# A Fourier transform and a top-1 mixture of experts in one kernel: the third batch's list in 19 blocks of 128, transforms that end eight blocks ahead, and the third batch's last part beside the list of two batches

## The chip, the cores and the metric

One NeuronCore of one Trainium2 chip runs the whole program. The metric is device time in microseconds (us). Engines: TensorE (PE, matmuls, and PEld for its weight loads), VectorE (DVE), ScalarE (ACT), GpSimd (POOL, which issues the indirect DMAs), SyncE (SP, which issues all other DMAs). Each engine works through its own instructions strictly in the order in which the program was built, so an instruction that waits holds back all that stands behind it on its engine.

## The reference

```python
def _attn_ref(x):                      # x: 8 x 2496 x 256
    X = np.fft.fft(x, axis=1)
    X = np.fft.fft(X, axis=2)
    return X.real.astype(np.float32)

def _moe_ref(x, modality_id, w_gate, modality_bias, w1, w2):   # x: 19968 x 256, 8 experts, F = 1024
    logits = x @ w_gate + modality_bias[modality_id]
    e_idx = np.argmax(logits, axis=1)
    probs = softmax(logits)
    gate_w = probs[np.arange(N), e_idx]
    for e in range(E):
        mask = e_idx == e
        h = np.maximum(x[mask] @ w1[e], 0.0)
        out[mask] = gate_w[mask, None] * (h @ w2[e])
```

Each of 8 batches of 2496 rows is Fourier transformed in both directions; each resulting row then goes through the one expert with the highest logit, two layers of 256 x 1024 and 1024 x 256.

## The kernel before, in words

**Transforms.** The transform of a batch is written as matmuls. Its input is loaded (`load_x`, L359) in two halves XM, folded on DVE (`fold`, L441 to L476), and put through `stage1` (L489, matmuls L506 or L508) and `stage23` (L515), which for each of 11 groups g makes a stage-2 product T2 (matmuls L532, L537 or L540) and, one group later, a stage-3 product (matmuls L550 or L552). Batches 0 to 2 use fp32 matmuls, batches 3 to 7 pairs of fp16 numbers (a high and a low part). Every product leaves PSUM in an evacuation: where pairs are made, ACT writes the high part (L486) and DVE the low part (L487). Of a stage-3 product, the 512 values of a row go into a row tile `rp` in this way, and the 16 gate logits are copied to `Lg` (L560). Six buffers (RPB) hold the `rp` tiles of even batches and batch 1.

**Routing.** `route` (L592) takes the logits to expert, gate weight and destination, on DVE for the most part. Each batch's rows are then scattered by 22 indirect DMAs on POOL (`scatter`, L669) into the HBM buffer `xd`, sorted by expert. Batch 0's are issued at once, those of later batches wait in a list `pend` and are issued a few at a time (`paced`, `trickle`).

**Weights.** `weights` (L775) loads each expert's fp32 weights (L802), and splits them into fp16 pairs on ACT and DVE (L812 to L844), which end up in SBUF and, by `wstore` (L797), in the HBM buffer `w16`.

**Expert blocks.** A block takes 256 or 128 rows of one expert (`block`, L963): SP loads the expert's weights from `w16` where they change (L987, L988), the rows transposed (xT, L990), and indices and gates (ig, L993). PE runs the first layer (L1006, 48 matmuls of 256 or 128 columns), ACT and DVE evacuate the hidden values H as fp16 pairs (L1011 and L1012; four evacuations a block of 256, two a block of 128), PE runs the second layer (L1024, 24 matmuls per 128 rows), ACT scales the result into a tile `ob` (L1030, two buffers) and POOL scatters it to the output (L1031, "outs").

Eight *speculative* blocks, one of 256 rows for each expert (`spec_blocks`), run as soon as batch 0 is routed, with the weights that have just been split. Then come *lists*: a list R takes as many full blocks as the rows of batches 0 to R-1 are sure to give (`table`, L875, on DVE). The first list, of two batches (R = 2), has blocks of 128 rows; the next six have 256; a last one takes what remains, in blocks of 128. While the blocks of list R run, the transforms of later batches are fed in between.

**What sets the order.** Python generators are stepped by hand. Up to the first list the string `SEQ` says which goes next: `w` a step of the weights, `s` a step of the transforms, `b` half a speculative block. In the lists, `knots` (L1056) reads from the points `pts` (L1113) how far the transforms (`k.pos`) should be after `at` units of 256 rows. A scheduler then places the instructions of each engine, with the order of stepping as priority.

Of the kernel before, what the change touches and what calls it, by code (L numbers as in the profile page):

```python
# [13 lines left out]
F32 = mybir.dt.float32  # L14
# [16 lines left out]
ROW = 516  # L31
RW = 516
CH = 3
RPB = 6
RPL = 4
HIP = ()
HIV = ()
# [19 lines left out]
NSLOT = 2  # L57
NS2 = 3
LEAD = 2
EARLY = -1  # L60
FIRST = 2
WAB = 4
WFB = 1
# [10 lines left out]
UB = 2  # L74
RV = 1
FG = 6
SEQ = "wsssssssswssssswssswsssssssssssssssssssssssssswssssbsswssswsssssbwsssssbsssssbwsssswsbwsswssswsssssbwbsssssbsssssbwsssssbwsssssbwsssssbwssssswwssssssssswssssswsssssssssss"
PARTS = ((0, 3), (3, 5))
XE = 1
M2 = 1  # L80
# [145 lines left out]
class Kernel:  # L226
# [288 lines left out]
    def stage23(self, b):  # L515
# [8 lines left out]
        for g in range(G + 1):  # L524
# [19 lines left out]
            if g > 0:  # L544
                T2 = T2s[g - 1]
                ps3 = self.psf.tile([P, 512], F32, name="psf")
                for j, cols in enumerate((slice(0, 145), slice(145, 280))):
                    if hl:
                        for k, (a, w) in enumerate(HL):
                            nc.tensor.matmul(ps3[0:M3, cols], self.e3h[:, a, j, :], T2[:, w, cols], start=k == 0, stop=k == 2)  # L550
                    else:
                        nc.tensor.matmul(ps3[0:M3, cols], self.e3[:, j, :], T2[:, cols], start=True, stop=True)  # L552
                j = (g - 1) % CH
                if j == 0:
                    pool, n = (self.rows, RPL) if b >= SPB and b % 2 else (self.rt, RPB)
                    self.rp.append(pool.tile([M3, CH, RW], I16, name="rp", bufs=n))
                row = self.rp[-1].bitcast(F16)[:, j, 0:512].rearrange("p (h s c) -> p h s c", h=2, c=64)
                seg = ps3[0:M3, 0:288].rearrange("p (s c) -> p s c", c=72)
                self.evac(row, seg[:, :, 0:64], 2.0 ** -20 if hl else self.inv[0][:M3])
                nc.vector.tensor_copy(Lg[:, g - 1], seg[:, 0:3:2, 64:72])  # L560
            yield

    def modality(self):
# [399 lines left out]
    def block(self, S, ti, i, o=0, n=0, ex=None):  # L963
# [62 lines left out]
        gs = p.tile([P, NT], F32, name=f"gs{S}", bufs=3)  # L1026
        V.tensor_scalar(gs, ig[:, :, 1], w2[:, 4 * F:4 * F + 2].bitcast(F32), None, ALU.mult)  # L1027
        for tg in range(NT):
            ob = p.tile([P, D], F32, name="ob", bufs=2)
            self.ob = nc.scalar.activation(ob, po[:, tg, :], AF.Identity, scale=gs[:, tg:tg + 1]).ins  # L1030
            ins = nc.gpsimd.indirect_dma_start(  # L1031
                out=t["out"], out_offset=bass.IndirectOffsetOnAxis(ap=ig.bitcast(I32)[:, tg, 0:1], axis=0),
                in_=ob, in_offset=None, bounds_check=TOK - 1, oob_is_err=False).ins
            tc.declare_no_dep(ins, group="out_w", reason="rows are disjoint")
            tc.add_to_no_dep_group("out_w", ins)
            if self.started:
                self.trickle(ins)
# [27 lines left out]
def fft_moe(ctx, tc, t):  # L1065
# [28 lines left out]
    k.w1.append(p.tile([P, 4 * F], F16, name="w1_y", bufs=1))  # L1094
    k.w2.append(p.tile([P, WROW - 4 * F], F16, name="w2_y", bufs=1))
    k.nslot = NS2
    while k.ready < R0 - 1:
        next(st, None)
    for _ in blk:
        k.paced()  # L1100
        for i in range(3):
            next(st, None)
            k.paced()
    k.started = True

    R0 = FIRST
    size = lambda R: P if R == R0 else 256
    starts, taken = {R0: 0}, k.ntaken
    for R in range(R0, B):
        n = (R * N - taken - E * (size(R) - 1)) // size(R)  # L1110
        starts[R + 1] = starts[R] + n * size(R) / 256
        taken += size(R) * n
    pts = [(0, k.pos)] + [(starts[b] + EARLY, b + 1) for b in range(SPB, B)]  # L1113
    at = 0
    k.slots = lambda b: int(2 * (starts[b + 1] - LEAD - at))
    tab = k.table(size(R0), False, R0)
    for R in range(R0, B + 1):
        blk, nxt = k.blocks(size(R), tab, R), None
        for _ in blk:
            at += size(R) / 512  # L1120
            while k.pos < knots(at, pts) and next(st, END) is not END:
                pass
            if R < B and nxt is None and at >= starts[R + 1] - LEAD:
                while k.ready < R:
                    next(st)
                nxt = k.table(256, False, R + 1)
        tab = nxt
    run_all([k.blocks(128, k.table(128, True))])

# [54 lines left out]
```

## Time and profile before

| | us |
|---|---|
| median of 3 runs (1081.33 to 1083.68) | 1083.2 |
| the profiled execution | 1081.88 |
| its span, first to last instruction | 1080.1 |
| PE busy (10128 matmuls) | 1007.7 |
| DVE busy | 552.8 |
| ACT busy | 446.8 |
| POOL busy | 373.3 |

The profile shows one execution. In its groups a row gives line, engine, operation, out<-in with their shapes, count, then busy time, mean ns of one, and the engine's idle time just before them with what ended it. In timelines a row is start, duration, engine, line, operation, count, and in brackets the idle time before it with its releaser. Matmuls overlap, so PE's busy time is not PE at its full rate. The granted TensorE clock is a share of full speed.

### The profile page before, as it was taken

What the parts mean: (1) busy time and instruction counts of PE and PEld (TensorE: products, weight loads), DVE (VectorE), ACT (ScalarE), POOL (GpSimd) and SP (SyncE); (2) the same over time, 40 slices, a digit from 0 to 9 for tenths busy, and PEclk for the clock granted to TensorE, in tenths of its full rate; (3) what the DMA queues carried; (4) which work ended last, traced back from release to release, by engine and by line L of the source; (5) the groups of instructions that cost most, each with busy time, mean ns of one, the idle gap of its engine ahead of it and who ended that gap; (6) DMA issues with size and microseconds to landing.
All of it is one profiled execution on the core that took longest, in us unless ns stands there. A gap on an engine that the chain in (4) does not pass through costs nothing.

```text
span 1080.1 us, 26648 instructions
## 1 busy us (share of the span) xinstructions
PE 1007.7 (93%) x10128; PEld 910.1 (84%) x10128; DVE 552.8 (51%) x1620; ACT 446.8 (41%) x882; POOL 373.3 (35%) x351
## 2 busy tenths in 40 slices
PE   6776879889998999999999999999999999999996
PEld 5656868779888988889899999888888888899985
DVE  4878888978887442363565334732222222222221
ACT  6755767744644333333443343332323233233221
POOL 0072482861243334343334333345543112121111
PEclk9897989999999999999999999999999999999998
DMA  9667987799497979877878595849976886797663
GB/s 348 246 227 247 308 270 240 260 295 332 135 287 226 305 240 292 225 235 249 252 221 259 178 251 156 244 126 287 298 215 197 244 272 183 222 242 204 163 156 105
DMA packets 156484, 254.89 MB, mean 236 GB/s; under 512 B 118364, under 2 KB 121317, under 8 KB 136125
## 3 DMA queue, kind: packets, MB, share of 16 engines
q1 hardware_dynamic: 136973, 210.96, 66.7%
q0 software_dynamic: 19376, 42.16, 11.8%
q8 instruction: 82, 1.34, 0.5%
q14 instruction: 53, 0.43, 0.1%
HBM read 231.59 MB, written 60.48 MB: 270 GB/s over the span
## 4 chain that ended last, share of the span: by engine, by line
PE 64%; issue 13%; DMA 9%; DVE 5%; ACT 4%; POOL 3%; SPq 1%; POOLq 0%; ACTq 0%; DVEq 0%
PE psm L1006 29%; PE pso L1024 28%; DMA XM<-x 3%; DMA out<-ob,ig 3%; POOL out L1031 2%; PE psf L550 2%; PE psf L532 1%; PE psf L506 1%; ACT wj L812 1%; DVE XM L368 1%; DMA xd<-rp,dsti 1%; PE psf L508 1%; POOL xd L670 1%; DMA wa<-w 1%; DVE w L838 1%
## 5 line engine op out<-in xcount | busy, mean ns | idle before, releaser
L1024 PEld LDWEIGHTS <-H 128*128 128x128 f16 x3864 | 376.1, 98 | 55.7 <-ACT H L1011 10.3
L1031 POOL DMA_INDIRECT out<-ob,ig x161 | 166.6, 1035 | 583.2 <-ACT ob L1030 503.4
L1012 DVE SCALAR_TENSOR_TENSOR H<-psm,H 128x512 f16<-128x512 f32 x322 | 218.4, 686 | 282.7 <-ACT H L1011 281.4
L1006 PE MATMUL psm<-xT,w 128*128 128x256 f16 (+1 forms) x3216 | 315.0, 256 | 13.5 <-DMA xT<-xd 6.7
L1024 PE MATMUL pso<-w,H 128*128 128x256 f16 x2616 | 308.0, 273 | 10.7 <-ACT H L1011 9.0
L1006 PEld LDWEIGHTS <-w 128*128 128x128 f16 x3216 | 268.9, 99 | 41.3 <-issue 11.7
L1011 ACT ACTIVATE H<-psm 128x512 f16<-128x512 f32 x322 | 190.5, 597 | 239.8 <-PE psm L1006 238.7
L1030 ACT ACTIVATE ob<-pso,gs 128x256 f32<-128x256 f32 x161 | 70.7, 471 | 282.1 <-PE pso L1024 239.4
L1006 PE MATMUL psm<-xT,w_y 128*128 128x256 f16 (+1 forms) x1440 | 135.3, 251 | 0.5 <-DVE H L1012 0.4
L670 POOL DMA_INDIRECT xd<-rp,dsti x88 | 104.7, 1190 | 84.5 <-DVE sp_i L863 53.7
L1024 PE MATMUL pso<-w_y,H 128*128 128x256 f16 x1152 | 133.3, 273 | 0.0
L1006 PEld LDWEIGHTS <-w_y 128*128 128x128 f16 x1440 | 117.0, 98 | 11.0 <-issue 1.2
L670 POOL DMA_INDIRECT xd<-rm,dsti x88 | 93.3, 1060 | 28.5 <-issue 25.2
L487 DVE SCALAR_TENSOR_TENSOR T<-psf,T 120x280 f16<-120x280 f32 (+2 forms) x95 | 43.2, 461 | 56.3 <-ACT T L486 55.9
L1027 DVE TENSOR_SCALAR gs<-ig,w 128x2 f32<-128x2 f32 (+1 forms) x67 | 15.2, 227 | 63.2 <-DMA ig<-xd 63.2
L486 ACT ACTIVATE T<-psf 120x280 f16<-120x280 f32 (+2 forms) x95 | 38.6, 421 | 15.4 <-PE psf L532 10.2
L812 ACT ACTIVATE wj<-wa 128x1024 f16<-128x1024 f32 x32 | 34.3, 1072 | 9.5 <-DMA wa<-w 9.4
L550 PE MATMUL psf<-T,pack 120*117 120x145 f16 x330 | 31.8, 224 | 4.8 <-DVE T L487 3.0
L368 DVE TENSOR_TENSOR XM<-XM 128x1280 f32<-128x1280 f32 (+2 forms) x18 | 24.1, 1338 | 23.2 <-DMA XM<-x 23.2
L552 PEld LDWEIGHTS psf<-T,pack 120*117 120x117 f32 x132 | 19.4, 188 | 17.0 <-ACT T L482 11.2
L552 PE MATMUL psf<-T,pack 120*117 120x145 f32 (+1 forms) x132 | 23.4, 300 | 11.1 <-ACT T L482 7.5
L532 PE MATMUL psf<-pack,T 128*120 128x144 f16 (+1 forms) x330 | 32.2, 229 | 1.3 <-DVE Lg L560 1.3
(197 smaller groups left out, 772.8 us busy)
## 6 DMA issues: line engine op xcount, KB each, us to landing
w<-w SPq DMA_DIRECT2D x67, 1028.0 KB
w<-w SPq DMA_DIRECT2D x67, 1024.0 KB
w_y<-w SPq DMA_DIRECT2D x30, 1028.0 KB
w_y<-w SPq DMA_DIRECT2D x30, 1024.0 KB
XM<-x SPq DMA_DIRECT2D x14, 1280.0 KB
wa<-w SPq DMA_DIRECT2D x16, 1024.0 KB
out<-ob,ig POOLq DMA_INDIRECT x161, 6.3
w<-w_x SPq DMA_DIRECT2D x2, 1028.0 KB
```

Of the source, the lines that this page charges most:

```text
L487: self.mark = self.nc.vector.scalar_tensor_tensor(dst[:, 1], ps, scale, dst[:, 0], ALU.mult, ALU.subtract).ins
L532: nc.tensor.matmul(oh, T1[h][:, a, g, :], self.m2h[h][:, w], start=h + k == 0, stop=h * k == 2, skip_group_check=True)
L550: nc.tensor.matmul(ps3[0:M3, cols], self.e3h[:, a, j, :], T2[:, w, cols], start=k == 0, stop=k == 2)
L552: nc.tensor.matmul(ps3[0:M3, cols], self.e3[:, j, :], T2[:, cols], start=True, stop=True)
L670: i = self.nc.gpsimd.indirect_dma_start(out=self.t["xd"], out_offset=bass.IndirectOffsetOnAxis(ap=at, axis=0), in_=row, in_offset=None, bo ...
L812: nc.scalar.activation(jk, x, AF.Square, accum_out=st[:, i:i + 1])
L1006: l1 = nc.tensor.matmul(ps[:, q, :], w1v[:, h, kt, ft], xT[:, xs, :], start=k == 0, stop=k == 5).ins
L1011: nc.scalar.activation(H[:, 0, f0:f0 + NF, :], ps, AF.Relu)
L1012: self.mark = V.scalar_tensor_tensor(H[:, 1, f0:f0 + NF, :], ps, 0.0, H[:, 0, f0:f0 + NF, :], ALU.max, ALU.subtract).ins
L1024: nc.tensor.matmul(po[:, tg, :], H[:, hh, ft, tg * P:(tg + 1) * P], w2v[:, wh, ft, :], start=k == 0, stop=k == 23)
L1030: self.ob = nc.scalar.activation(ob, po[:, tg, :], AF.Identity, scale=gs[:, tg:tg + 1]).ins
L1031: ins = nc.gpsimd.indirect_dma_start(out=t["out"], out_offset=bass.IndirectOffsetOnAxis(ap=ig.bitcast(I32)[:, tg, 0:1], axis=0), in_=ob, i ...
```

## The change

Five things are changed together. Lines below the constants are one higher in the changed file.

1. `SEQ` is shorter: 82 `s` steps instead of 136, and the last `b` and `w` steps stand close together. Before the first list, the old kernel stepped the transforms until three batches were routed (and three more steps for each remaining half block); the new one steps until two are (one step for each). The point (1, max(3, k.pos)) then lets the rest of the third batch be stepped within the first two blocks of the first list.
2. The list of three batches (R = 3) is cut into blocks of 128 too (`SMALL = 4`). By the counts of `starts`, the lists were 15 blocks of 128, then 5, 10, 10, 10, 9 and 10 of 256, then 22 of 128 for these inputs; they are now 15 and 19 of 128, then 6, 9, 10, 10 and 10 of 256, then 21 of 128.
3. A batch's transform now ends eight units before the start of the list that needs it (`AHEAD`), instead of one unit before the start of the list ahead of that.
4. The logit copy to `Lg` goes from DVE to ACT.
5. `ob` has four buffers instead of two, `rp` five instead of six.

```diff
-RPB = 6
+RPB = 5
...
-EARLY = -1
+AHEAD = 8
+SMALL = 4
...
-SEQ = "wsssssssswssssswssswsssssssssssssssssssssssssswssssbsswssswsssssbwsssssbsssssbwsssswsbwsswssswsssssbwbsssssbsssssbwsssssbwsssssbwsssssbwssssswwssssssssswssssswsssssssssss"
+SEQ = "wsssssssswssssswssswsssssssssssssssssssssssssswssssbsswssswsssssbwsssssbsssssbwsssswsbwsswssswsssssbwbsbbwbwbwbwwwww"
...
-                nc.vector.tensor_copy(Lg[:, g - 1], seg[:, 0:3:2, 64:72])
+                nc.scalar.copy(Lg[:, g - 1], seg[:, 0:3:2, 64:72])
...
-            ob = p.tile([P, D], F32, name="ob", bufs=2)
+            ob = p.tile([P, D], F32, name="ob", bufs=4)
...
-    while k.ready < R0 - 1:
-        next(st, None)
     for _ in blk:
         k.paced()
-        for i in range(3):
-            next(st, None)
-            k.paced()
+        next(st, None)
+        k.paced()
+    while k.ready < 1:
+        next(st, None)
...
-    size = lambda R: P if R == R0 else 256
+    size = lambda R: P if R < SMALL else 256
...
-    pts = [(0, k.pos)] + [(starts[b] + EARLY, b + 1) for b in range(SPB, B)]
+    pts = [(0, k.pos), (1, max(3, k.pos))] + [(starts[b + 1] - AHEAD, b + 1) for b in range(SPB, B)]
...
-                nxt = k.table(256, False, R + 1)
+                nxt = k.table(size(R + 1), False, R + 1)
```

**ACT, in the speculative blocks.** Before, around the two outs' evacuations of the fourth such block (`ob<-pso`, L1030; `wj` is a square sum of the weights, `T` and `rp` are evacuations of the transform, DMASW are POOL's DMAs):

```order
L1030 ACTIVATE ob<-pso,gs_1750 128x256 [waits DMASW0_49,PE_49]
L1030 ACTIVATE ob<-pso,gs_1750 128x256 [waits DMASW1_49]
L1011 ACTIVATE H_1798<-psm 128x512 [waits PE_49]
L812 ACTIVATE wj,wst<-wa 128x1024 [waits Activation_49]
L1011 ACTIVATE H_1798<-psm 128x512 [waits PE_49]
L486 ACTIVATE rp<-psf,xsc 117x256 [waits PE_49]
L542 COPY T_1605<-psf 120x280 [waits PE_49]
```

And the same block's place in the changed kernel:

```order
L1031 ACTIVATE ob<-pso,gs_1750 128x256 [waits PE_49]
L1031 ACTIVATE ob<-pso,gs_1750 128x256
L1012 ACTIVATE H_1798<-psm 128x512 x2
L487 ACTIVATE rp<-psf,xsc 117x256 [waits PE_49]
L543 COPY T_1605<-psf 120x280 [waits PE_49,Activation_49]
L1012 ACTIVATE H_1798<-psm 128x512 [waits PE_49]
L475 ACTIVATE XM<-Pt,xsc 128x640 [waits DVE_49]
L475 ACTIVATE XM<-Qt,xsc 128x640 [waits DVE_49]
L813 ACTIVATE wj,wst<-wa 128x1024 [waits Activation_49]
L487 ACTIVATE rp<-psf,xsc 117x256 [waits PE_49]
L561 COPY Lg<-psf 117x16 [waits DVE_49] x2
```

These two ob evacuations no longer wait for POOL's DMAs, and two logit copies, which wait for DVE, have come in behind a row's evacuation.

**DVE, at the first list block.** Before, from the gate scale `gs` of the first list block to its two evacuations (`H_3086`):

```order
L1027 TENSOR_SCALAR gs_3266<-ig_3084,w_0_106 128x1
L487 SCALAR_TENSOR_TENSOR T_2887<-psf,T_2887 120x280
L475 SCALAR_TENSOR_TENSOR XM<-Pt,xsc,XM 128x640
L475 SCALAR_TENSOR_TENSOR XM<-Qt,xsc,XM 128x640
L487 SCALAR_TENSOR_TENSOR rp<-psf,rp 117x256
L560 COPY Lg<-psf 117x16
L487 SCALAR_TENSOR_TENSOR T_2968<-psf,T_2968 120x280
L1012 SCALAR_TENSOR_TENSOR H_3086<-psm,H_3086 128x512
L487 SCALAR_TENSOR_TENSOR rp<-psf,rp 117x256
L560 COPY Lg<-psf 117x16
L1012 SCALAR_TENSOR_TENSOR H_3086<-psm,H_3086 128x512
```

In the changed kernel, around the same block's two (`H_2663`; L461 to L470 are half of a fold, here of batch 4's input):

```order
L462 TENSOR_TENSOR XM<-XM 128x635
L461 TENSOR_TENSOR XM<-XM 128x5x127
L466 COPY Qt<-XM 128x5
L468 TENSOR_TENSOR Pt<-XM 128x5x63
L470 TENSOR_TENSOR Qt<-XM 128x5x63
L465 COPY Pt<-XM 128x5
L467 TENSOR_TENSOR Pt<-XM 128x5x64
L469 TENSOR_TENSOR Qt<-XM 128x5x64
L1028 TENSOR_SCALAR gs_2863<-ig_2661,w_0_106 128x1
L1013 SCALAR_TENSOR_TENSOR H_2663<-psm,H_2663 128x512 x2
L488 SCALAR_TENSOR_TENSOR T_2978<-psf,T_2978 120x280
L369 TENSOR_TENSOR XM<-XM 128x1280
```

Before, the last T2 and row evacuations of batch 3 stood ahead of the first list block's H; now batch 3's T2 evacuations begin behind it, and the logit copies are gone from DVE.

More of the change, by code (lines that the diff above doesn't have):

```diff
@@ L1096, in fft_moe @@
     k.nslot = NS2
-    while k.ready < R0 - 1:
-        next(st, None)
     for _ in blk:
         k.paced()
-        for i in range(3):
-            next(st, None)
-            k.paced()
+        next(st, None)
+        k.paced()
+    print('POS', k.pos, len(k.pend))
+    while k.ready < 1:
+        next(st, None)
     k.started = True
     R0 = FIRST
-    size = lambda R: P if R == R0 else 256
+    size = lambda R: P if R < SMALL else 256
     starts, taken = {R0: 0}, k.ntaken
```

## The prediction

> **What bounds the kernel now.** I read the page's slices first, then three windows cut where the work changes (first speculative block, first list block, end of the first list, last matmul), then the waits and timelines of VectorE (DVE), ScalarE (ACT) and TensorE (PE) in the first of them. In the slices each digit is the busy share of 27 us in tenths; look at where PE reaches 9 and where DVE leaves 7 to 8.
>
> ```profile
> PE   6776879889998999999999999999999999999996
> DVE  4878888978887442363565334732222222222221
> ```
>
> The windows: busy time and, in brackets, instructions of each engine, then granted clock, DMA share, GB/s.
>
> ```profile
> 94.00:238.00 144.00, 125.82 (x1121) 110.24 (x1120) 121.64 (x372) 91.46 (x167) 76.92 (x58) 0.92 0.88 279
> 238.00:346.00 108.00, 100.44 (x1387) 95.65 (x1385) 93.45 (x323) 55.84 (x121) 32.29 (x29) 0.98 0.83 241
> 346.00:1071.00 725.00, 719.09 (x7297) 652.09 (x7296) 273.00 (x714) 238.60 (x472) 235.20 (x236) 1.00 0.79 226
> ```
>
> From 346 us on PE is busy 719 of 725 us: nothing is to be gained there but by less PE work. From 94 to 238 us the eight speculative blocks run beside the transforms of batches 2 and 3 and the weight preparation. DVE is busy 121.6 of 144 us there, ACT 91.5. PE is marked busy 125.8, but 768 MoE matmuls are only 84 us of it at the full rate that these chain rows give (start, us, what):
>
> ```profile
> 255.98 2.68 PE psm L1006 x48
> 258.66 2.62 PE pso L1024 x24
> ...
> 425.92 3.93 PE psm L1006 x36
> ...
> 432.14 4.26 PE pso L1024 x39
> ```
>
> A block of 128 is 2.68+2.62 = 5.30 us. Of a block of 256, 36 first-layer matmuls take 3.93 and 39 second-layer ones 4.26, so 0.109 us each and 10.48 for the 96. So the first 238 us hold the loss, and DVE is nearest to being the bound there. PE's total work hardly changes; the time falls by as much as the first list block starts earlier, less the PE work that is moved behind that start.
>
> **Part 1: DVE work that leaves the stretch before the first list block.** In the DVE order I counted between the first speculative block's H evacuation and the first list block's. Gone from there are 11 T2 evacuations, 9 row evacuations, 20 logit copies, 4 splits of L475 and half a batch's fold (L368, L460, L461, L466 to L469 once each).
>
> ```profile
> L487 DVE SCALAR_TENSOR_TENSOR T<-psf,T 120x280 f16<-120x280 f32 x55 | 24.1, 440 | 33.1 <-ACT T L486 32.9
> L487 DVE SCALAR_TENSOR_TENSOR rp<-psf,rp 117x256 f16<-117x256 f32 x55 | 22.8, 414 | 5.1 <-ACT rp L486 5.1
> L560 DVE COPY Lg<-psf 117x16 f32<-117x16 f32 x88 | 14.2, 161 | 0.0
> L475 DVE SCALAR_TENSOR_TENSOR XM<-Pt,xsc,XM 128x640 f16<-128x640 f32 x10 | 8.8, 880 | 1.1 <-ACT XM L474 0.9
> L368 DVE TENSOR_TENSOR XM<-XM 128x1280 f32<-128x1280 f32 x14 | 20.8, 1484 | 15.3 <-DMA XM<-x 15.3
> L460 DVE TENSOR_TENSOR XM<-XM 128x635 f32<-128x635 f32 x12 | 9.7, 808 | 0.0
> L466 DVE TENSOR_TENSOR Pt<-XM 128x320 f32<-128x320 f32 x12 | 5.8, 480 | 0.0
> ```
>
> 11 x 0.440 + 9 x 0.414 + 20 x 0.161 + 4 x 0.880 + (1.48 + 2 x 0.81 + 4 x 0.48) = 20.3 us. Neighbours on DVE overlap by some 0.06 us, which takes 3 us off, and about as much comes back from small pieces (a row copy, the steps of a table): 20 us, read as that much earlier since DVE hardly rests there. What goes later with them: 1 x load on SP, 20 scatters on GpSimd (POOL), and PE work, part 4.
>
> **Part 2: ob in four buffers.** Two outs of ob queue on POOL behind scatters, so ACT stands for a free ob, and behind it in ACT's order stand the H evacuations that DVE and PE wait for. ACT's rows, then DVE's:
>
> ```profile
> 155.08 0.47 ACT L1030 ACTIVATE ob<-pso,gs 128x256 f32<-128x256 f32 x1 [5.57 <-DMA out<-ob,ig]
> 156.69 0.47 ACT L1030 ACTIVATE ob<-pso,gs 128x256 f32<-128x256 f32 x1 [1.14 <-DMA out<-ob,ig]
> ...
> 225.75 0.47 ACT L1030 ACTIVATE ob<-pso,gs 128x256 f32<-128x256 f32 x1 [3.00 <-DMA out<-ob,ig]
> ```
>
> ```profile
> 157.69 0.69 DVE L1012 SCALAR_TENSOR_TENSOR H<-psm,H 128x512 f16<-128x512 f32 x1 [2.51 <-ACT H L1011]
> 159.21 0.69 DVE L1012 SCALAR_TENSOR_TENSOR H<-psm,H 128x512 f16<-128x512 f32 x1 [0.83 <-ACT H L1011]
> ...
> 226.75 1.30 DVE L1012 SCALAR_TENSOR_TENSOR H<-psm,H 128x512 f16<-128x512 f32 x2 [3.94 <-ACT H L1011]
> ```
>
> DVE idles 2.51+0.83+3.94 = 7.3 us for them. With four buffers an ob waits for the out of two blocks back, and the last speculative outs have almost no scatters ahead of them in the new POOL order. I take 7 us, bounds 0 and 7.3. Late next is what DVE lacks in the other 15 us of its idle time, the speculative blocks' ig loads and the weights' ScalarE half among it.
>
> These stalls also cool PE: in the window around the first one the clock is 0.86, and 12 first-layer matmuls take 2.77 us, 11 of them later 1.36.
>
> ```profile
> 135.00:162.00 27.00, 20.20 (x164) 17.83 (x162) 22.00 (x54) 17.12 (x32) 21.81 (x18) 0.86 0.90 271
> ```
>
> ```profile
> 161.89 2.77 PE L1006 MATMUL psm<-xT,w 128*128 128x256 f16 x12
> ...
> 168.60 1.36 PE L1006 MATMUL psm<-xT,w 128*128 128x256 f16 x11
> ```
>
> The Trainium skill, "TensorE: Matmul & The Clock Gate", section "Part 1: The HAM clock gate", says the clock falls to half after an idle window of about 3.4 us; the trace agrees in that the 2.77 us stand behind a wait of PE of 5 us for that H. By the rule the removed stall also gives back PE speed, at most 0.14 x 27 = 3.8 us here, and the sum would be that much lower if PE set the pace. DVE does, so my sum has nothing for it.
>
> **Part 3: the logit copy on ACT.** It is 0.16 us on DVE; on ACT it must wait until DVE has done its half of the same evacuation. Queued behind it on ACT are T2, row and H evacuations, and DVE, then PE, wait for those. ACT has 52 us free in the first window, so its own time costs nothing. In the new ACT order one to six instructions mostly stand between a row's evacuation and its copy, and DVE mostly has over 1 us of other work before it needs ACT's next piece; for eight or so of the 33 copies ahead of the first list it has less than ACT's pieces take (by the mean durations of the trace), by 7 us together. Bounds 0 and 7, I take +3. With parts 1 and 2 the first list block, now at 237.7, starts 24 us earlier, near 214.
>
> **Part 4: PE work moved and added.** Ahead of the first 128-column matmul PE's order had 60 stage-2 and 49 stage-3 matmuls of batch 3, and now 10 and 0; 28 second-layer matmuls of the last speculative block follow it too. Six of stage 2 or 3 take 0.38 to 0.39 from start to start:
>
> ```profile
> 344.12 0.53 PE L550 MATMUL psf<-T,pack 120*117 120x145 f16 x6
> 344.50 0.56 PE L532 MATMUL psf<-pack,T 128*120 128x144 f16 x6
> 344.89 0.54 PE L550 MATMUL psf<-T,pack 120*117 120x145 f16 x6
> ```
>
> 99 x 0.064 + 28 x 0.109 = +9.4. Blocks: 15, 19 and 21 of 128 and 45 of 256 in place of 15 and 22, and 54. 18 x 5.30 - 9 x 10.48 = +1.1.
>
> **Part 5: inside the lists.** In the first list PE idles 7.6 of 108 us now. DVE's work there stays about the same (2 us less), but it no longer enters the list behind. I take -2, bounds -7.6 and 0. Loads: the second of batch 4's x loads now stands in SP's queue between the weights of the first and second list blocks, 1.28 MB where DMA is already full.
>
> ```profile
> 245.00:250.00 5.00, 5.00 (x70) 4.72 (x68) 3.84 (x14) 1.85 (x4) 1.33 (x1) 1.00 1.43 355
> ```
>
> At 355 GB/s that is 3.6 us; +3, bounds 0 and 5. The 19-block list begins with three blocks that all take new weights, at 5.3 us a block beside transforms. The last list begins so today, with little else on the DMA, and PE's waits from 940 us on hold only
>
> ```profile
> PE psm L1006 <- DMA w<-w: 2.5, 2, 1.4
> ```
>
> so I take +2, bounds 0 and 8. The Trainium skill, same page, section "HAM oscillation", tells of thin matmuls (M=128) whose DMA waits of 3 to 5 us bring half clock each time; here the thin blocks of the first and last lists run at 5.30 us each, and by the rule the sum would only change if those waits came (rival D).
>
> At nothing: rp in five buffers makes batch 1's evacuations wait one tile sooner for batch 0's scatters, some 2 us at most; the cover is the first speculative block, which waits for the last of those scatters anyway (its landing, then the block's ig):
>
> ```profile
> 87.42 2.89 DMA xd<-rm,dsti
> 94.20 4.01 DMA ig<-xd
> ```
>
> Transforms that end eight blocks ahead leave 8 x 10.48 = 84 us for two dozen scatters of some 1.3 us; without that cover PE would wait at a list's start.
>
> **Sum**, against the profiled execution's 1081.9 (span 1080.1): -20 -7 +3 +9.4 +1.1 -2 +3 +2 = -10.5, so 1071.4. The median of the three runs, 1083.2, lies 1.3 above that execution: **1073**. All good ends give -24, all bad ones +10.
>
> **Rivals.** A, slower: ACT and DVE fall into lockstep over the logit copies. Place: 33 copies before the first list and 22 in it. For it: the 7.3 us show that DVE stands as soon as ACT does. Against: the other work between. Without part 3 the sum is -13.5, so it decides at 13.5/55 = 0.25 us a copy; at 0.5 us it adds 27.5 and the time is 1097.
> B, no gain: DMA, not DVE, sets the first list's start. 144 us at 279 GB/s are 40.2 MB; one x load and 20 scatters (120 KB each) less leave 36.5 MB, which at the same rate take 131 us: 13 earlier instead of 24, and the sum is +0.5, time 1084; with a little more rate 1080. For it: a DMA share of 0.88. Against: 355 GB/s in the row above.
> C, faster: with DVE ahead, the first list runs without its 7.6 us of idle time and no load is late: 1073 - 5.6 - 5 = 1062.
> D: the first three blocks of the 19-block list each wait 3.5 us for weights and run 3.4 us at half clock, 3 x 5.2 = 15.6 in place of 2: 1087. Against: the 2.5 us above.
>
> **How the numbers follow.** Forecast 0.52 (1066 to 1080), C 0.20, B 0.13, A 0.10, D 0.05. The range 1062 to 1085 leaves out A, D and what of C lies below 1062, together under 0.2. 0.2% (2 us) is about what a measurement of this kernel can tell from no change: faster 0.52 + 0.20 + 0.05 of B = 0.77, same the other 0.08 of B, slower A and D, 0.15.
>
> **What would show it.** First list block near 214 us; no ACT wait of several us for ob before it; DVE busier than 0.85 from 94 us to there; PE idle in the first list at most 7 us; no waits for weights over 3 us at the 19-block list. I am wrong if DVE's idle time there grows behind ACT (A), if DVE waits for DMA (B), or if the first list starts earlier and the gain is gone by the end of the second.

## The result, and the profile after

The changed kernel takes 1099.06 us (median of 4 runs, 1096.74 to 1105.20) beside 1083.44 us of the kernel before in the same session: ratio 1.0151, 95% interval [1.0103, 1.0199]. It is slower, where 1073 us and a faster kernel were forecast. The profiled execution takes 1098.41 us with a span of 1096.6, so 16.5 us more than the 1080.1 of before. Three single executions in the experiments below, of 3531 us (`a_rm4`), 2668 us (`b_seq`) and 1150 us (`a_ig9`), lie above the others of their kernel and are in no ratio.

The slices of the changed kernel, to be read against those of before. Each is 27.4 us here. PE's long run of 9s begins no earlier (the tenth slice in both), and PE falls to 8 again in the 14th and 16th slices (356 to 384 and 411 to 439 us), where before it was full. DVE is thinner in the first ten slices and stays at 6 to 9 one slice longer.

```profile
PE   6675979889999898999999999999999999998996
DVE  4777687976987634773323633382322222222221
```

The windows of the changed kernel, cut at the fifth speculative block, the first list block, the start and end of the 19-block list and the start of the last list (us, busy time and instructions of PE, PEld, DVE, ACT and POOL, granted clock, DMA share, GB/s):

```profile
95.00:168.50 73.50, 60.19 (x485) 53.01 (x485) 57.55 (x173) 44.01 (x88) 31.90 (x27) 0.88 0.85 270
168.50:228.60 60.10, 52.96 (x502) 46.75 (x499) 48.99 (x141) 38.65 (x70) 12.88 (x11) 0.94 0.77 251
228.60:349.50 120.90, 112.77 (x1529) 106.36 (x1530) 95.68 (x314) 60.94 (x151) 42.23 (x37) 0.99 0.92 262
349.50:481.30 131.80, 120.70 (x1638) 114.56 (x1636) 73.58 (x211) 55.67 (x128) 49.79 (x48) 0.99 0.82 225
481.30:964.40 483.10, 483.10 (x4529) 434.69 (x4527) 178.24 (x458) 159.51 (x326) 175.16 (x177) 1.00 0.85 243
964.40:1085.00 120.60, 116.63 (x1545) 109.88 (x1544) 31.92 (x62) 36.26 (x66) 22.91 (x24) 0.99 0.77 190
```

From 481 to 964 us PE is busy all of the time. The 19-block list has 11 us without PE. Ahead of the first list PE is busy 113.2 of 133.6 us and DVE 106.5, a share of 0.80: DVE did not become the busier engine that the forecast wanted (over 0.85).

Busy time still contains slow matmuls, so I use a second measure. **PE's lost time** at a block is the block's start less all matmul work that PE has done by then, each matmul counted at its spacing in undisturbed runs: 2.68/48 and 0.109 us for the expert blocks, as in the prediction, 0.064 for stages 2 and 3, and so on for the other forms of the transform. A stretch in which lost time stays flat is limited by PE alone. What is taken for those other forms shifts the numbers by up to some 3 us, in both kernels alike, so the differences between the kernels count, not the level. Start and lost time, both in us:

| at the start of | before: start | lost | after: start | lost |
|---|---|---|---|---|
| first speculative block | 94 | 44.3 | 95 | 45.4 |
| fifth speculative block | 167 | 65.2 | 169 | 68.1 |
| first list block | 237.7 | 77.9 | 228.6 | 78.5 |
| third batch's list (256 before, 128 after) | 352 | 89.7 | 349.5 | 91.9 |
| the same work later (19 blocks of 128, or 9 of 256) | 447 | 90.7 | 481.3 | 106.5 |
| first block of the last list | 945 | 93.4 | 964.4 | 106.4 |
| its last block shown | 1062 | 96.2 | 1078 | 111.6 |

Lost time at the end differs by 111.6 - 96.2 = 15.4 us, and with the 1.1 us of added matmuls that is the 16.5. Two things stand out. The first list starts 9 us earlier, but its lost time is the same, so the 9 us are the PE work that was moved behind it (start less lost: 159.8 before, 150.1 after). And the 19-block list loses 14.6 us where the blocks of 256 in its place lost 1.0.

Where did the stalls for ob go? None is left ahead of the first list. Three rows of waits of the kernel before, from 94 to 238 us (total us, times, longest):

```profile
ACT ob L1030 <- DMA out<-ob,ig: 10.5, 4, 5.6
ACT wj L812 <- DMA wa<-w: 3.6, 4, 1.4
DVE H L1012 <- ACT H L1011: 8.9, 5, 3.9
```

In the changed kernel from 95 to 228.6 us, first DVE's waits, then ACT's, and the longest of PE's (from 94 to 228 us):

```profile
DVE H L1013 <- ACT H L1012: 10.0, 10, 3.5
DVE rm L208 <- DMA xd<-rm,dsti: 9.6, 1, 9.6
```

```profile
ACT wj L813 <- DMA wa<-w: 14.3, 5, 5.1
ACT Lg L561 <- DVE tb_t L925: 10.1, 1, 10.1
```

```profile
PE psf L387 <- ACT Lg L561: 6.9, 1, 6.9
```

DVE waits for ACT's half of H for as long as before (10.0 us, 8.9 before). New are the 9.6 us for an rm buffer, the 10.1 us that ACT stands with a logit copy behind it, the 6.9 us that PE then stands, and most of ACT's 14.3 us for raw weights.

DVE's order of the changed kernel around the long one shows how it comes about:

```profile
128.69 0.06 DVE L909 MEMSET tb_v<- 1x1 f32 x1
138.33 0.20 DVE L208 COPY rm<-tail 117x4 int32<-117x4 int32 x1 [9.58 <-DMA xd<-rm,dsti]
```

DVE reaches the copy of the fourth row group (`rows`, L208) at 128.75 us and waits until 138.33 for one of three rm buffers, which a scatter on POOL must read first. Before, the same copy ran at 137.55 without a wait. DVE had been busy for 36.2 us since 94 us when it came there before, and for 30.9 us since 95 us now: it had less ahead of it, came early, and stood until about the time at which it had come before.

### The profile page after: what moved, and what is told of

Its sections match the earlier page's. It is cut to its first block, busy times and chain, and to the rows that moved or that the text cites. A ratio compares the mean times of both kernels' runs of the same rounds, so it can differ in the third digit from the quotient of the medians.

```text
span 1096.6 us, 27711 instructions
## 1 busy us (share of the span) xinstructions
PE 1011.2 (92%) x10560; PEld 918.5 (84%) x10560; DVE 548.3 (50%) x1541; ACT 458.0 (42%) x970; POOL 363.8 (33%) x351
## 4 chain that ended last, share of the span: by engine, by line
PE 62%; issue 12%; DMA 8%; DVE 7%; ACT 5%; POOL 3%; SPq 1%; POOLq 0%; ACTq 0%; DVEq 0%
PE psm L1007 29%; PE pso L1025 28%; DMA w<-w 2%; POOL out L1032 2%; DMA wa<-w 2%; DMA xd<-rp,dsti 1%; PE psf L551 1%; DMA xd<-rm,dsti 1%; POOL xd L671 1%; PE psf L533 1%; ACT wj L813 1%; DVE H L1013 1%; DMA out<-ob,ig 1%; PE psf L507 1%; DMA pack<-c_pack 1%
## 5 line engine op out<-in xcount | busy, mean ns | idle before, releaser
L1032 POOL DMA_INDIRECT out<-ob,ig x161 | 162.2, 1008 | 598.2 <-ACT ob L1031 527.0
L1007 PEld LDWEIGHTS <-w 128*128 128x128 f16 x3504 | 272.6, 99 | 28.2 <-DMA w<-w 4.7
L1007 PE MATMUL psm<-xT,w_y 128*128 128x128 f16 (+1 forms) x1584 | 137.4, 246 | 3.4 <-DMA w_y<-w 3.4
L1007 PEld LDWEIGHTS <-w_y 128*128 128x128 f16 x1584 | 121.6, 99 | 12.1 <-DMA w_y<-w 4.0
L671 POOL DMA_INDIRECT xd<-rp,dsti x88 | 95.2, 1082 | 89.8 <-ACT T L483 55.3
L671 POOL DMA_INDIRECT xd<-rm,dsti x88 | 97.7, 1110 | 33.9 <-issue 25.8
L1028 DVE TENSOR_SCALAR gs<-ig,w 128x1 f32<-128x1 f32 (+1 forms) x73 | 16.0, 219 | 63.2 <-DMA ig<-xd 63.2
L533 PEld LDWEIGHTS <-T 128*120 128x120 f16 x330 | 26.9, 134 | 10.1 <-issue 8.2
L551 PEld LDWEIGHTS <-pack 120*117 120x117 f16 x330 | 27.2, 134 | 7.8 <-issue 7.5
L488 DVE SCALAR_TENSOR_TENSOR rp<-psf,rp 117x256 f16<-117x256 f32 x55 | 21.8, 415 | 20.3 <-ACT rp L487 20.3
```

The source lines that it names most:

```text
L488: self.mark = self.nc.vector.scalar_tensor_tensor(dst[:, 1], ps, scale, dst[:, 0], ALU.mult, ALU.subtract).ins
L533: nc.tensor.matmul(oh, T1[h][:, a, g, :], self.m2h[h][:, w], start=h + k == 0, stop=h * k == 2, skip_group_check=True)
L671: i = self.nc.gpsimd.indirect_dma_start(out=self.t["xd"], out_offset=bass.IndirectOffsetOnAxis(ap=at, axis=0), in_=row, in_offset=None, bo ...
L1007: l1 = nc.tensor.matmul(ps[:, q, :], w1v[:, h, kt, ft], xT[:, xs, :], start=k == 0, stop=k == 5).ins
L1032: ins = nc.gpsimd.indirect_dma_start(out=t["out"], out_offset=bass.IndirectOffsetOnAxis(ap=ig.bitcast(I32)[:, tg, 0:1], axis=0), in_=ob, i ...
```

## The experiments

Ratios are to the kernel before on the same chip in the same session, with 95% intervals. The runs come from five sessions. In three of them the kernel before takes 1083 to 1084 us, in the first it takes 1113 and in the last 1118; the headings give that time. The expectations speak of chips, but the same chip number stands with a session at 1084 and with the one at 1118, so it is not shown that the difference is one between chips. The changed kernel itself was run at 1083 to 1084 us only; what differs from it by one part stands at about its ratio in the two others. Lost times are read from each run's own trace.

### Undoing one part at a time (kernel before at 1113 us)

```diff
a_small3:  -SMALL = 4                                  +SMALL = 3
a_lgdve:   -nc.scalar.copy(Lg[...], seg[...])          +nc.vector.tensor_copy(Lg[...], seg[...])
a_oldseq:  SEQ and the steps behind it as before
b_ob4 (kernel before):  -RPB = 6                       +RPB = 5
                        -name="ob", bufs=2             +name="ob", bufs=4
```

Third list in blocks of 256 again:

> The changed kernel with the list of three batches back at blocks of 256, all else as changed. Theory: the trace of the changed kernel loses some 14 us more than its matmuls need inside the 19-block list (matmul work 115.5 us, 130 us from its first to its last block), so most of that should come back: 1099 - 10 to 13 = 1086 to 1089, and the first list block still starts near 229 us. Rival (the logit copy on ScalarE makes the engines wait for each other wherever transforms run beside blocks): the transforms run beside the list of any block size, so 1097 to 1100.

1.0035 [1.0015, 1.0055]. Against the changed kernel's 1.0122 to 1.0151 the 19-block list costs some 0.9 to 1.2%, as the first theory had it, but without it the rest of the change still gains nothing.

Logits on VectorE again:

> The changed kernel with the logit copy back on VectorE, all else as changed. Theory: the copy costs what the trace shows of waits for it, at most 0.4 us of TensorE in the first list and 4.7 us in the 19-block list; the 6.9 us wait ahead of the first list is the rm-buffer wait seen through it; so 1094 to 1098. Rival (lockstep over the copy is the cause of the loss): 1080 to 1086, and the first list block starts near 214 us.

1.0142 [1.0092, 1.0192]: the logit copies on ACT are not the cause. Rival A of the prediction falls.

The kernel before with four ob buffers:

> The kernel before with only the buffers changed: ob four, rp five. Theory: the ScalarE waits for a free ob ahead of the first list (10.5 us) go, the first list block starts 6 to 10 us earlier, 1074 to 1078. Rival (VectorE has other waits that fill the place at once): 1082 to 1085.

0.9978 [0.9951, 1.0005]: at most half a per cent, and not clear of no gain at all. ACT no longer waits for ob ahead of the first list in this trace, and of the 7 us that the prediction took for these stalls about 2 came back as time.

The old order of steps with all else changed:

> The changed kernel with the old SEQ and the old run-up to the first list (three batches routed before it), all else as changed. Theory: the 9.6 us wait of VectorE for an rm buffer and most of the 14 us of ScalarE waits for weight loads come from the shorter SEQ; without it the gain of the ob buffers stays and the 19-block list still loses 10 to 15: 1085 to 1091. Rival (the order of steps is harmless, the loss is the logit copy or the list): 1097 to 1100.

1.0134 [1.0083, 1.0184]: the new order neither causes the loss nor brings a gain, to within half a per cent, which is how far this interval reaches.

### What the 19-block list loses its time to (kernel before at 1084 us)

The changed kernel itself again, as the reference of this group:

> The changed kernel itself, beside the runs with one thing undone, so that the four share a chip. On the first chip it took 1.0151 [1.0103, 1.0199] times the time of the kernel before. Every theory expects the same here, 1.010 to 1.020, and the 15 blocks of work lost between the start of the 19-block list and its end (14 to 20 us beside none in the five 256-blocks of before).

1.0122 [1.0058, 1.0186]. First list block at 225.1 us, lost 74.9; the 19-block list loses 18.2 us (89.9 to 108.1). Over six runs of this list with its loads the loss is 12.0 to 18.2 us, mean some 15.8, so this trace is the highest of them.

The list's weight loads skipped while the program stays as it is:

```diff
+        if R == 3:
+            V.memset(tb[:, 2, :], 0.0)          # table: no block needs new weights
-        first = i < ns
+        first = i < ns and self.nread != 3
```

> The changed kernel with the 19-block list's own weight loads left out: its table says that no block needs new weights, so every conditional load is skipped while the order of all instructions stays as it is (the blocks then multiply with stale weights). Theory W (the list loses its 14 to 15 us to the weight loads: PE waits for them, runs at half clock behind, and the transforms' own transfers queue behind them): the list loses at most 4 us and the ratio to the kernel before falls from 1.015 to 1.002 to 1.005. Theory C (the transforms' matmuls stand in runs of 6 to 59 between the thin blocks, where PE waits for T2 and row evacuations): only the one wait of 3.6 us and the half clock behind it go, 4 to 6 us, ratio 1.009 to 1.011, and PE still waits for T, rp or Lg beside the list.

1.0055 [1.0026, 1.0085]; the list loses 8.6 us. PE's waits in this list, first in the changed kernel (`a_same`), then with the loads skipped:

```profile
PE psm L1007 <- DMA w<-w: 5.0, 1, 5.0
PE psf L533 <- ACT Lg L561: 4.9, 4, 2.3
PE psf L551 <- DVE T L488: 2.4, 3, 1.2
```

```profile
PE psf L533 <- ACT Lg L561: 2.7, 3, 2.3
PE psf L551 <- DVE T L488: 2.4, 3, 1.2
```

The wait for weights goes, and with it a slow block. In the changed kernel's own profile that block reads (start, us):

```profile
435.69 4.34 PE L1007 MATMUL psm<-xT,w 128*128 128x128 f16 x48 [3.60 <-DMA w<-w]
439.82 2.97 PE L1025 MATMUL pso<-w,H 128*128 128x256 f16 x24
442.63 2.84 PE L1007 MATMUL psm<-xT,w_y 128*128 128x128 f16 x48
```

48 matmuls take 4.34 us behind a wait of 3.60 and 2.84 one block later; the granted clock from 435.6 to 440.0 us is 0.63. Waits of PE for psf, the transforms' PSUM buffers, stay: the transforms' matmuls stand in runs of 6 to 59 between the thin blocks, and each run stops for its evacuations on ACT and DVE.

The same loads taken out of the program, so that the scheduler knows that none comes:

```diff
-        if ex is None:
+        if ex is None and self.nread != 3:
             wsrc = t["w16"][ds(ee, 1)]...
```

> The changed kernel with the 19-block list's weight loads taken out of the program (stale weights again). The scheduler, which no longer expects a wait there, then places the 19 blocks one behind the other and the transforms' matmuls among the 256-blocks that follow. Theory C: both causes are gone, the list loses 1 us or less and the ratio is 1.000 to 1.004, 6 to 10 us below the run that only skips the loads. Theory W: as with the loads skipped, the two within 0.2% of each other. A third case, that 128-blocks lose their time by themselves: the list still loses 10 us and the ratio stays over 1.010.

1.0029 [1.0004, 1.0055]; the list loses nothing at all:

```profile
353.50:455.70 102.20, 102.20 (x1394) 97.05 (x1392) 37.27 (x81) 35.16 (x70) 45.73 (x46) 1.00 0.42 105
```

PE is busy 102.20 of 102.20 us. Here the scheduler put 19 blocks one behind the other and the transforms among the 256-blocks that follow, which lost 3.9 us (96.4 to 100.3; those of the kernel before lost 2.7). So thin blocks lose nothing by themselves. Against the 18.2 us of `a_same`, 9.6 go with the loads (the wait, the slow clock, later starts), against the mean of six runs some 7; the other 8.6 go with the transforms' runs. As time, skipping the loads gave 7.8 us (medians 1098.34 and 1090.54), and taking them out of the program only 3.0 more (1087.51), a step that the two intervals do not separate: what the list no longer loses is in part lost behind it. That the transforms' runs vanish from between the blocks when the program has no loads speaks for this: the scheduler expects a wait for weights after each change of expert and fills it with transforms. In the trace PE then waits for weights in one place only, and the filling has waits of its own.

### What sets the stretch ahead of the first list (kernel before at 1083 to 1084 us)

Five traces of the changed order (after, `a_same`, and the runs above and below that change nothing ahead of the first list: `a_skipw`, `a_nowload`, `a_skip1`) have the first list block at 225.1 to 231.5 us, lost 74.9 to 81.4. Only what falls outside these ranges counts as a shift; their means are 228.4 and some 78.

```diff
a_norow:    paced():  -for group, _ in self.pend[:1]: group.rows()
a_lessdma:  wstore(): +skipped for experts 3 to 7;  table(): +expert = min(expert, 2)
a_skip1:    table():  +if R == 2: V.memset(tb[:, 2, :], 0.0)
a_rm4:      -RMB = 3   +RMB = 4;  ob in 3 buffers;  wj in 8 bits
```

Rows prepared later:

> The changed kernel in which the paced scatters no longer prepare the rows of the group behind the next one, so DVE reaches a row copy later and should not stand 9.6 us for one of three rm buffers, nor ACT 10.1 us behind it for the logits. Theory R (these two stalls are what ate the gain of the shorter DVE work ahead of the first list): the first list block starts 5 to 10 us earlier, ratio 1.006 to 1.010. Rival (the stretch is paced by the scatters and transfers, and the stall only shows where DVE had time to lose): the first list starts within 2 us of where it does in the changed kernel, ratio 1.013 to 1.017.

1.0123 [1.0058, 1.0187], first list block at 225.5 us. This run tells nothing: the scheduler moved the row copy up again, and DVE's wait for rm is still 8.9 us in its trace.

Four rm buffers:

> The changed kernel with four rm buffers in place of three (ob in three buffers, the junk output of the weights' squares in 8 bits, to make room). DVE's wait of 9 us for an rm buffer, and ACT's and PE's behind it, go. Theory E: the first list block starts 5 to 9 us earlier, near 220, and the ratio is 1.004 to 1.009. If the stretch is paced by something else (transfers, the scatters on GpSimd), the time comes back as other waits: start within 3 us of 225 to 231, ratio 1.010 to 1.016.

1.0131 [1.0089, 1.0172], first list block at 226.8 us, lost 77.6. Now the wait is gone, and nothing is won at the first list. PE's waits of this run from 95 to 226.8 us show what came instead:

```profile
PE psm L1007 <- DVE H L1013: 8.9, 5, 3.4
PE psm L1007 <- DMA xT<-xd: 6.9, 1, 6.9
PE pso L1025 <- ACT H L1012: 5.6, 2, 3.9
```

So theory E, that the rm stall ate the gain, falls for the stretch as a whole. Inside it something did move: the fifth speculative block starts at 159.5 us here and at 164.8 in `a_rm4_small3` below, against 167.4 to 170.7 in eight runs of the changed order with three buffers. From there to the first list block the two then take 67 us, where the others take 53 to 62. DVE's work moved likewise: it is busy 51.4 us up to the fifth block and 57.1 behind it, 57.7 and 48.9 in the changed kernel, so how much of the shift is the buffers' alone is open.

Ten MB less to move:

> The changed kernel in which the prepared weights of experts 3 to 7 are not written out (10 stores of 1 MB, of 36 MB that move between 95 and 226 us), every instruction's place kept; the lists then load the weights of the first three experts in their place. Theory D (transfers set the first list's start, rival B of the prediction): the first list block, at 225 to 231 us in five runs of the order as it is, starts 10 us or more earlier, and the ratio to the kernel before is 1.006 or less. Theory E (the engines' order sets it: DVE stands 9 us for an rm buffer, PE 7 us behind it, ACT 11 us for raw weights): the first list block within 4 us of there, ratio 1.009 to 1.015.

1.0095 [1.0065, 1.0125], first list block at 221.3 us, lost 71.1.

```profile
95.00:221.30 126.30, 114.58 (x985) 100.80 (x983) 105.75 (x313) 83.23 (x155) 45.87 (x37) 0.92 0.63 191
```

The DMA share falls from 0.81 to 0.63 and some 7 us are won, of the 37 that ten MB take at the 268 GB/s of that stretch in `a_same`. That is less than theory D's 10 us and more than theory E's 4, with a ratio in E's range: transfers have a part in the stretch, a small one. Rival B of the prediction had the list's start nearly right (13 us earlier; it was 9) and its cause wrong: at 7 us for ten MB, its 3.7 MB less would be some 2.6 us, so it was near by luck.

The first list without its conditional loads:

> The changed kernel in which the first list's conditional weight loads are skipped by its table (the first load of each slot stays; stale weights otherwise), every instruction's place kept. The list lost 13 to 16 us from its first to its last block. If weight loads cost it what they cost the 19-block list (about half of its loss), 6 to 8 us go and the ratio is 1.005 to 1.008. If the loss is all in the transforms' runs between the blocks, 2 us or less go, ratio 1.010 to 1.014.

1.0124 [1.0086, 1.0162]; the first list loses 11.8 us in place of 13 to 16. So most of its loss is not in the loads; that it is in the transforms' runs is what is left, not shown.

All this together with the third list in blocks of 256:

> The same with the third list in blocks of 256 again, so what is left of the change is the earlier end of the transforms, ob in three buffers, rp in five, the logits on ACT. The 19-block list costs 10 to 15 us (1.0 to 1.3%), so with the gain of theory E the ratio is 0.993 to 0.998, faster than the kernel before; without it 0.999 to 1.004.

1.0036 [1.0012, 1.0059]: as `a_small3`, no gain.

Then cuts of about equal size on one engine each, and the new order of steps alone in the kernel before:

```diff
a_lesspe:   speculative blocks: 4 of 6 and 16 of 24 products of each kind
a_lessdve:  +if e < 3:  V.scalar_tensor_tensor(lo, x, s, hi, ...)
a_lessact:  squares of x[:, 0:64] in place of x[:, 0:1024] for e >= 3
b_seq:      kernel before with the new SEQ and the steps behind it
```

> The changed kernel whose eight speculative blocks leave out one of the three products of each layer (256 of 768 matmuls, 28 us of PE work at 0.109 us each). Theory F (ahead of the first list PE's work and the chain of blocks through it set the pace, so removed DVE work turns into waits): the first list block, at 225 to 231 us in five runs of the order as it is, starts 18 to 28 us earlier. Theory G (DVE sets the pace, as predicted): it starts at most 8 us earlier.

1.0056 [1.0031, 1.0080]; first list block at 228.5 us. 28 us less of PE work, and the list starts where it did: for the stretch as a whole theory F falls. Up to the fifth speculative block it holds: that starts at 154.1 us, 13 to 17 us earlier than in the runs of the changed order with all products, and four blocks have 14 us less of matmuls. From there to the first list block the run takes 74.4 us, and the gain is gone. So PE's work is on the path of the first half, and something else, not found here, sets the end of the second. By the ratios the kernel as a whole is 7 to 10 us faster than the changed one: some 5 us less matmul work lies behind the list's start, and the lists lose less.

> The changed kernel in which DVE leaves out the low halves of the weights of experts 3 to 7 (25 to 30 us of DVE work ahead of the first list; stale low halves instead). Theory G: the first list block starts 20 to 30 us earlier. Theory F: at most 8 us earlier.

0.9994 [0.9968, 1.0020]; first list block at 221.2 us.

```profile
95.00:221.20 126.20, 113.29 (x990) 99.46 (x990) 92.03 (x314) 85.25 (x161) 39.50 (x37) 0.94 0.89 293
```

DVE is busy 92.0 us here, 14 less than in `a_same`, not 25 to 30: the scheduler has put other DVE work, folds of the transform among it, into the room. Its share is 0.73. The list starts about 7 us earlier, where theory G wanted 20 or more and F at most 8. But the first list then loses 6.3 us (70.8 to 77.1) where it lost 13 to 17 in the other runs of the changed order, with DVE busy for 79.3 us in it in place of 95.9 in `a_same`, and the kernel is some 15 us faster than the changed one. About half of the cut of DVE's work is paid out, half of that behind the point at which the forecast looked for it. As the transforms are placed differently in this run, the half is not all DVE's.

> The changed kernel in which ScalarE squares 64 of 1024 columns of the raw weights of experts 3 to 7 (some 18 us of ACT work less; another scale for these weights). Theories F and G both: at most 5 us earlier. A third case, that the preparation of weights on ACT, which waits 11 us for raw weights, sets the pace: 10 us or more earlier.

1.0168 [1.0117, 1.0219]; first list block at 231.3 us. No gain from ACT, which is busy 72.3 us up to there in place of 83.0 in `a_same`.

> The kernel before with the new order of steps ahead of the first list and nothing else (two ob buffers, logits on VectorE, third list in blocks of 256, transforms ending one block ahead). The prediction's part 1 by itself: the first list block, at 237.7 us in the kernel before, starts near 218, and the time falls by 20 - 9.4, ratio 0.988 to 0.993. Theory F: it starts about 9 us earlier, by the PE work that is moved behind it, and the time stays, ratio 0.998 to 1.004.

0.9992 [0.9964, 1.0021]; first list block at 226.3 us, lost 75.1. It starts 11 us earlier, as theory F had it, by 9 us of moved PE work and little more, and the time stays. This is the prediction's part 1 by itself, forecast at 10.6 us of time, and it gives nothing, to within some 4 us.

### SP's queue, and what is left as a faster version (kernel before at 1118 us)

SP's own queue stands too. Its largest waits in `a_same` from 95 to 226 us:

```profile
SPq L798 <- DVE w L839: 21.5, 5, 9.5
SPq L994 <- DMA out<-ob,ig: 20.6, 3, 14.1
```

The 14.1 us are the load of an ig (L994) that needs one of four buffers, which an out of a speculative block has yet to read (the second block's, not the first's as the expectation says); raw weights and transposed loads stand behind it. Nine buffers take that wait away.

```diff
-        ig = p.tile([P, NT, 2], F32, name=f"ig{S}", bufs=4)
+        ig = p.tile([P, NT, 2], F32, name=f"ig{S}", bufs=9)
```

> The changed kernel with the token lists of the outs (ig) in nine buffers in place of four, so that SP's queue no longer stands 14 us for an out of the first speculative block before it can issue the next transposed load and raw weights. PE loses 21 to 23 us between the first and the fifth speculative block, in the kernel before and in the changed one alike. Theory S (SP's queue sets this first half): the loss there falls by 8 us or more, the fifth block starts at 160 us or earlier in place of 168, and the ratio to the kernel before is 1.008 or less. Rival (blocks, scatters and weights hand over to one another, as in the other cuts): the fifth block starts within 4 us of 168, ratio 1.010 to 1.016.

1.0138 [1.0111, 1.0165]; fifth speculative block at 172 us, as in the other runs of sessions at 1113 and 1118 us (171 to 173). Theory S falls for the ig wait. SP's stores of prepared weights (L798), which wait 22.0 us for DVE in this run too, were not taken away, so SP's queue as such is not ruled out.

> The kernel before with ob in four buffers (rp in five, as in the change) and ig in nine: what might be left as a faster version. Theory S: 8 us or more of the loss between the first and the fifth speculative block go, ratio 0.990 to 0.994. Rival: ratio 0.996 to 1.001, as with ob in four buffers alone (0.9978 [0.9951, 1.0005]).

0.9956 [0.9934, 0.9979]: faster than the kernel before by 0.2 to 0.7%, and the only version here that is clear of it. Its parts ahead of the first list lose what `b_ob4` loses (94.5 and 94.2 us at the first list block, each in its session), and its interval overlaps that of `b_ob4`, so a gain beyond ob's four buffers is not shown.

## Why the prediction was wrong, point by point

**Where the 27 us are.** Forecast was -10.5 on the profiled execution, measured +16.5. By the tables: the first list block was to start at 214 and started at 228.6 (14.6 us); the 19-block list was to cost 2 and cost 13.6 (11.6 us); the first list's +1 was +1.6, and the rest nearly cancels (the lists of 256 lost 2.7 before and nothing after, the last list 2.4 more).

**The step that failed first** is in part 1: "20 us, read as that much earlier since DVE hardly rests there". It stood in the sum without bounds. Two rows of before, cut at the fifth speculative block, show what should have been asked:

```profile
94.00:167.00 73.00, 62.33 (x498) 54.70 (x497) 58.38 (x180) 47.30 (x87) 33.97 (x28) 0.89 0.95 294
167.00:238.00 71.00, 63.49 (x626) 55.54 (x624) 63.26 (x193) 44.16 (x80) 42.95 (x30) 0.95 0.81 263
```

The count of removed DVE work was right: from the H evacuation of the first speculative block to that of the first list block the durations of DVE's instructions add up to 145.7 us before and 125.5 after. But DVE's busy time there fell by 15.7 us (120.4 to 104.7), and its idle time grew from 21.0 to 29.6. And PE was no looser than DVE: the prediction set the 84 us of MoE matmuls against the 144 us and left out the transforms' matmuls; with them PE had 110 us of work there (159.8 - 49.7, start less lost at both ends).

Against the changed kernel's first two rows above, DVE's work up to the fifth block is the same (58.4 and 57.6 us), and all that was removed came out of the second half (63.3 to 49.0). In that half PE had lost only 77.9 - 65.2 = 12.7 us: 58.3 of its 71 us were PE work. With 9.4 us of that moved behind the list, the half could shrink by 22 us at the very most, and only if PE then never waited. It shrank by 10.9, to 60.1 us, of which PE still loses 10.4. The 21 to 23 us that PE loses in the first half were out of part 1's reach, since it took no DVE work from there. DVE was the busiest engine beside PE by the window, but not the one that sets the pace: cutting 25 to 30 us of its work (14 us of its busy time there) moved the list's start by 7, 28 us of PE work by nothing, some 11 us of ACT's busy time by nothing, 10 MB of transfers by 7. No one engine's work is paid out in full at the list's start. That each hands over to the next through few buffers in fixed orders, and the next wait takes what one cut frees, fits all of these runs, but no run shows it as the only reading.

**Part 2, the ob stalls (-7).** They went, as said. But the rm wait of 9.6 us, which came with the change, and ACT's waits for raw weights (3.6 us before, 14.3 after) stand in their place. Alone, in the kernel before, four buffers are worth at most half a per cent.

**Part 3, logits on ACT (+3).** No difference could be measured, to within half a per cent, and rival A is refuted by `a_lgdve`. A small trace of it is in the 19-block list, where PE waits 4.9 us for psf buffers that the logit copy on ACT frees last.

**Part 4** held: PE work ahead of the first list block fell by 9.7 us for the 9.4 worked out, and the blocks' 1.1 are in the sum of the result.

**Part 5, the 19-block list (+2, bounds 0 and 8).** The sum looked at its first three blocks and at weights alone; rival D (+15.6) had nearly the right size with the wrong place. The first three blocks lose 2 us. The loss is spread: one wait for weights of 3.6 to 5.0 us at the fourteenth block with a slow clock behind it, and 8 to 9 us in the transforms' runs. The prediction priced the list by the last one, which has next to no transforms in it; the nearer row was the first list of the kernel before, 15 thin blocks beside transforms, which lost 89.7 - 77.9 = 11.8 us. The Trainium skill, "TensorE: Matmul & The Clock Gate", section "HAM oscillation", warns of thin matmuls at half clock behind DMA waits; the trace agrees at that block (4.34 us for 2.84 and 2.97 for 2.78), which is 1.7 of the 14.6 us. What the sum had no term for is how the scheduler interleaves: beside blocks of 256 it lays transforms in runs of mostly 18 matmuls or fewer, inside the blocks and between them, beside blocks of 128 in runs of up to 59 between them.

**The rivals.** None of them was the case in which the first list starts earlier only by the PE work that is moved behind it, though the windows above would have priced it: 9.4 us earlier, nothing won. "The first list starts earlier and the gain is gone by the end of the second" stood there as a way to be wrong, without a price.

**Open.** What sets the start of the first list was not found: neither rm, ig, transfers nor one engine's work does by itself. The fifth speculative block came earlier with four rm buffers and with less PE work, and both times the stretch behind it took the gain back. The earlier end of the transforms (`AHEAD`) was not undone by itself; `a_small3` and `a_rm4_small3` lie 0.35% above the kernel before, and which of the parts left in them costs that is open. Where the gain of `b_ob4_ig9` arises was not traced.

## What to carry to other kernels

Before counting work that is taken off a busy engine as time, count what the engine that carries the end of the chain has lost in the same stretch, cut finely enough that the removed work and the lost time are in the same window: the gain cannot exceed that, but for work that moves out of the window. Count all work of that engine, not that of one part of the program. In this kernel a stall that was removed from a stretch in which PE, DVE and ACT run at 0.6 to 0.85 mostly turned into another; try a cut on each engine before believing in one of them. Where a scheduler fills expected waits, ask what it will put there and what that waits for: a list of small blocks that change weights often invites work into gaps that the hardware may not have.

## What was not expected of the hardware

The same kernel took 1083 to 1084 us in some sessions and 1113 to 1118 in others. In the slower ones PE's lost time keeps rising inside the lists of 256, where it is flat in the others: in `a_ig9` 129.3 at one block and 140.5 twenty blocks later, in `a_same` 108.1 and 108.0. PE's waits of `a_ig9` from 520 to 940 us, where `a_same` has none at all:

```profile
PE pso L1025 <- issue: 10.7, 23, 0.9
```

These are 23 stops of up to 0.9 us for which the profile shows no cause. Whether the chip or the session makes the difference is not shown.
